# Four hand-written orders of work made anew in a fused attention, FFN and routed-expert kernel

## The chip, the cores and the metric

The kernel runs on one core of one Trainium2 chip. The metric is the device time of one execution in microseconds: the median of the runs of the kernel before is 764.94 us (three runs, 762.08, 764.94 and 765.34).

## What is computed

```python
# attention, B=4, H=8, 512 local and 32 global positions, D=64
s_g = scale * np.matmul(q_g, k_all.transpose(0, 1, 3, 2)); out_g = np.matmul(sm(s_g), v_all)
mask = np.abs(pos[:, None] - pos[None, :]) <= 32          # local queries: a window, and all globals
s_l = np.concatenate([s_lg, np.where(mask, s_ll, -1e9)], axis=-1)
out_l = np.matmul(sm(s_l), np.concatenate([v_g, v_l], axis=2))
x = concatenate([out_g, out_l], axis=2) as (2176, 512) rows
# FFN, 512 to 2048 to 512
x = (np.maximum(x @ w_in, 0.0) ** 2) @ w_out
# routed experts, 8 of 512 to 1024 to 512
xc = x[x @ w_skip > 0]; logits = xc @ w_gate
e_idx = argmax(logits); gate_w = softmax(logits)[e_idx]
out = x.copy(); out[x @ w_skip > 0] = xc + gate_w * (np.maximum(xc @ w1[e], 0) @ w2[e])
```

## The kernel before

The 2176 rows are 16 tiles of 128 local tokens and one tile of the 128 global queries. The FFN takes the local tiles two at a time, in 8 blocks of 256 tokens. Most products are made in two parts: a tensor is split into a high part in float32r and the low rest, and three matmuls (high by high, high by low, low by high) stand for one. Block 0 works in plain float32 while the weights are still arriving. Attention for block j+1 runs beside the FFN of block j, and the routing of block j-1's tiles too. After block 7 the FFN of the global tile, its routing, and the first expert's two tiles follow; then the experts' tiles, under branches on the token counts.

The order of all this is written out by hand in four strings of tokens, each token one step. Every engine executes its instructions in the order in which the tokens emit them, and the DMA queues of SP, ACT and POOL too. SEQ (L21, read by `do`, L897) covers the start: loads, preparation, blocks 0 and 1 of the FFN, attention of tiles 0 to 5. EVEN (L31) is run for blocks 2, 4 and 6, ODD (L36) for 3, 5 and 7 (L953). TAIL (L41) is read by the loop at L997.

The tokens:
- F, E (and I, H in SEQ, which put the low part on VectorE instead of POOL): one FFN unit, alternately a first product (L664 to L666: 12 matmuls of 256 columns) and a second (L685 to L687: 12 of 512). F and I square on VectorE, E and H on ScalarE. The digit in SEQ is the block.
- a, b: a step of local attention for the block's two tiles. Step 1 is the scores (L387: 128 matmuls) with the softmax of one half (L396 to L403), step 2 the softmax of the other half, steps 3 and 4 transposes (L412), step 5 the product with v (L421), step 6 the transposes of the result.
- g: a step of global attention, four steps for each half of the heads: products with the keys (L453), transposes (L473), products with the values (L486: 40 matmuls), transposes of the result. Only the even blocks have them.
- q, 0 to 3, G: transposes of queries and keys. r, s, t: a step of the routing of one tile (t: the global tile): transposes (L270) and a bf16 copy; the other two thirds of the rows (L564 to L566) on VectorE; L586, the logits, and a chain of small VectorE operations; L611, L612 and a second chain that ends in two one-hot matrices (L633, L637); L640, the slot table, and the store of the rows to DRAM.
- W in SEQ: a transfer of 512 KB of FFN weights on SP's queue. A: puts the words of one chunk together, ScalarE (L211) and VectorE (L215, L219, L225). C, D: splits a chunk of weights, the low part on POOL (C) or VectorE (D). V, lv, lk, lq, lg and L: other loads on SP's queue.
- In TAIL: T is a step of the global tile's FFN (six matmuls of 512 columns, some with transposes). X and Y are steps of the first expert's tiles 0 and 1. W and w fetch 512 KB of expert weights, on ACT's queue and on SP's. C and c split a weight; the low part of the weight before (L794) goes to VectorE (C) or POOL (c). O opens places and issues two gathers (L817, POOL's queue), S makes the slot rows, gEJ gathers for expert E's tile J, pEJ transposes and splits what was gathered.

Of the kernel before, what the change touches and what calls it, by code (L numbers as in the profile page):

```python
# [18 lines left out]


SEQ = """  # L21
    Lk00 Lk01 Lg0 W P00 0G P01 Lq0 A L9 W Lq1 03 P0 00 V 0q 01 02 A W P1 0a W 0a W V 0a W A W 0b 0a A V 0b 0a 0b V A
    0a 0b W V W A 0b W A W W 0b 1q V A E0 A I0 W W W A 1a D W A 1a W F0 A 1a A D W E0 W H0 I0 A 1a 1b 1a W V A H0 A
    W H0 D A W E0 W D 1a F0 W 1b I0 Lg1 F0 A D V A W 1b E0 1b W A H0 D 1g A 1b C Lv00 V F0 1g E0 A A H0 H0 E0 A 1b C
    1g D D F0 Lq2 W Lv01 D H0 A 1g V W H1 H1 A A W H0 W H1 Lk10 1g A H1 H0 W 1g F1 2G D V A C C A I1 21 W 1g D H0 D
    E1 20 I0 D A Lq3 D H1 1g F0 A I0 I0 2q Lk11 D C E0 E0 A D 22 E0 C 23 F0 C C E1 R00 2a H1 R00 E1 2a R01 H1 2a R00
    R01 E1 I1 F1 C R00 2b R01 F1 2a D F1 2b 2a F1 V Lv10 D F1 H1 R01 R00 A D 2b H1 H1 C 2a I1 C E1 C V H1 F1 2b C I1
    F1 I1 H1 R01 2b E1 D 2b H1 V V
"""

EVEN = """  # L31
    E E q E a r a F E r E s E r E E s g E a s E a E a g F F r a F lg r V E g lv1 b s F g F E F b F F b b F E s V F
    lk1 V E g b F g F b g F F F g lq lk0 V F
"""

ODD = """  # L36
    q E E E G E 3 0 F E 2 r lq E r 1 F F r E a lv0 r E F s F r E s a F s a F F E b F a b F s E E a F E b V V b E E b
    a F F V s E b F F F V
"""

TAIL = """  # L41
    w T T r T r r s T T s T s W r w T T r T s C C T c s w T T T C W O W T c C W T p00 C w C T p01 w W T W W X X
    t C X t X t C X X t c X X X t S g02 g10 X Y Y Y W W Y W W p02 p10 Y W W Y Y W Y Y Y Y
"""

WARM = 8
# [1071 lines left out]
```

## Time and profile before

| | |
|---|---|
| median of 3 runs | 764.94 us |
| the profiled execution | 761.9 us, span 760.2 us |
| TensorE matmul busy | 720.3 us (95%) |
| TensorE weight load busy | 595.3 us (78%) |
| VectorE, ScalarE, POOL busy | 425.6, 394.9, 178.1 us |
| mean granted clock of TensorE | 0.991 |
| DMA | 95.32 MB, mean 125 GB/s |

Busy time is the sum of an engine's instruction times; weight loads run beside matmuls. The span goes from the first to the last instruction. A timeline row says in brackets how long the engine stood idle before the instruction and what ended that; "issue" means that no semaphore did. From 171.80 us on, a block of the main loop takes 59 to 65 us; block 7 ends at 528.90, and the experts behind the branches begin at 594.60.

### The profile page before, as it was taken

Reading aid. Unit: us, or ns where it says so; the run is one execution under the profiler, and the core shown is the slowest. Engines: PE = TensorE matmul, PEld = TensorE weight load, DVE = VectorE, ACT = ScalarE, POOL = GpSimd, SP = SyncE. Lnnn points to the kernel's source line nnn. Section 1 sums busy time; section 2 is a strip of 40 time slices with the busy share of each in tenths; the row PEclk is TensorE's granted clock in tenths of the full one; section 3 lists DMA queues with packets and bytes.
Section 4 is the critical chain, followed back from the end, with each engine's and each line's share of the span. In section 5 each row is a group of like instructions: output and inputs, shape, how many; then the busy total and the mean of one; then the engine's idle time right before and its main releaser. Section 6 shows DMA issues by size and latency. Waiting matters only on the chain. (4 is left out here: it accounts for less than half of the span.)

```text
span 760.2 us, 18565 instructions
## 1 busy us (share of the span) xinstructions
PE 720.3 (95%) x7443; PEld 595.3 (78%) x7443; DVE 425.6 (56%) x1072; ACT 394.9 (52%) x970; POOL 178.1 (23%) x209
## 2 busy tenths in 40 slices
PE   6789999999899999999999999999889998999897
PEld 4566776888788989878988888888577777887775
DVE  2889894954551652753174464241875289327881
ACT  5767566546345554533654634433453277326771
POOL 5000033231111111111212111221032243414431
PEclk9899999999999999999999999999999999999999
DMA  9999921142525113063304050001473699417700
GB/s 271 228 331 259 242 71 35 41 102 42 127 66 125 35 33 78 19 148 79 79 31 102 2 150 30 28 29 44 152 250 106 241 328 325 149 48 258 275 26 30
DMA packets 117396, 95.32 MB, mean 125 GB/s; under 512 B 83125, under 2 KB 90293, under 8 KB 117284
## 3 DMA queue, kind: packets, MB, share of 16 engines
q1 hardware_dynamic: 105856, 69.50, 34.2%
q10 hardware_dynamic: 8548, 16.00, 6.1%
q0 software_dynamic: 2880, 8.33, 3.3%
q8 instruction: 69, 1.13, 0.6%
q14 instruction: 43, 0.35, 0.1%
HBM read 82.08 MB, written 12.85 MB: 125 GB/s over the span
## 5 line engine op out<-in xcount | busy, mean ns | idle before, releaser
L176 POOL TENSOR_TENSOR gl<-g,gh 128x256 fp32r<-128x256 f32 x105 | 79.6, 758 | 339.4 <-ACT gh L175 177.7
L664 PE MATMUL h<-xh,w_in 128*128 128x256 f32 x448 | 131.1, 293 | 0.0
L666 PE MATMUL h<-xh,w_in 128*128 128x256 f32 x448 | 125.2, 279 | 0.0
L665 PE MATMUL h<-xl,w_in 128*128 128x256 f32 x448 | 125.2, 279 | 0.0
L685 PE MATMUL acc<-w_out,gh 128*128 128x512 f32 x224 | 93.5, 417 | 0.3 <-issue 0.3
L668 ACT ACTIVATE g<-h 128x256 f32<-128x256 f32 x128 | 48.7, 380 | 85.6 <-PE h L666 66.0
L687 PE MATMUL acc<-w_out,gl 128*128 128x512 f32 x224 | 88.7, 396 | 0.1
L686 PE MATMUL acc<-w_out,gh 128*128 128x512 f32 x224 | 88.4, 395 | 0.0
L664 PEld LDWEIGHTS h<-xh,w_in 128*128 128x128 f32 x448 | 84.1, 188 | 3.6 <-ACT gh L700 0.3
L665 PEld LDWEIGHTS h<-xl,w_in 128*128 128x128 f32 x448 | 84.3, 188 | 2.1 <-issue 0.3
L666 PEld LDWEIGHTS h<-xh,w_in 128*128 128x128 f32 x448 | 84.0, 188 | 0.0
L403 ACT ACTIVATE sm<-sm,mx 128x128 f32<-128x128 f32 x128 | 49.9, 391 | 64.5 <-DVE mx L401 62.9
L175 ACT CAST gh<-g 128x256 fp32r<-128x256 f32 x112 | 45.4, 406 | 29.0 <-DVE g L698 26.9
L396 DVE TENSOR_TENSOR sm<-sc,mask 128x512 f32<-128x512 f32 x32 | 21.9, 686 | 60.2 <-PE sc L387 56.6
L687 PEld LDWEIGHTS acc<-w_out,gl 128*128 128x128 f32 x224 | 42.0, 188 | 11.6 <-POOL gl L176 1.2
L176 DVE TENSOR_TENSOR ehl<-ertr,ehl 128x512 fp32r<-128x512 f32 x28 | 19.4, 692 | 50.8 <-ACT ehl L175 50.8
L685 PEld LDWEIGHTS acc<-w_out,gh 128*128 128x128 f32 x224 | 42.1, 188 | 6.9 <-issue 0.8
L686 PEld LDWEIGHTS acc<-w_out,gh 128*128 128x128 f32 x224 | 42.2, 188 | 5.8 <-issue 0.3
L848 ACT ACTIVATE er<-eh 128x512 f32<-128x512 f32 x28 | 16.7, 598 | 44.4 <-PE eh L845 44.4
L698 DVE TENSOR_TENSOR g<-h,g 128x256 f32<-128x256 f32 x46 | 19.3, 419 | 31.5 <-ACT g L668 31.3
L683 PE MATMUL acc<-st_raw_out,gh 128*128 128x512 f32 x64 | 31.6, 615 | 2.8 <-DVE st_raw_in L215 2.8
L817 POOL DMA_INDIRECT xg<-x2d,slots x20 | 24.2, 1208 | 38.2 <-DVE xp L176 8.6
(701 smaller groups left out, 1631.2 us busy)
## 6 DMA issues: line engine op xcount, KB each, us to landing
st_e<-in_moe_w_dram SPq DMA_DIRECT2D x50, 512.0 KB, 7.7
vr<-in_v_l_dram SPq DMA_DIRECT2D x56, 192.0 KB, 4.5
st_raw_in<-in_moe_w_in_dram SPq DMA_DIRECT2D x16, 512.0 KB, 9.4
st_raw_out<-in_moe_w_out_dram SPq DMA_DIRECT2D x16, 512.0 KB, 7.5
st_e<-in_moe_w_dram ACTq DMA_DIRECT2D x14, 512.0 KB, 7.0
x2d<-x ACTq DMA_DIRECT2D x17, 256.5 KB, 2.9
st_gv<-in_v_l_dram SPq DMA_DIRECT2D x8, 512.0 KB, 4.8
out_dram<-x ACTq DMA_DIRECT2D x16, 256.0 KB, 3.3
```

Source lines behind the costliest of these rows:

```text
L175: nc.scalar.copy(hi, src)
L176: (lo_engine or nc.vector).tensor_tensor(out=lo, in0=src, in1=hi.bitcast(F32), op=ALU.subtract)
L403: nc.scalar.activation(sm[:, hh, :], sm[:, hh, :], AF.Exp, bias=mx[:, hh:hh + 1], scale=SCALE, accum_out=osum[:, 2 * hh + g:2 * hh + g + 1],)
L664: nc.tensor.matmul(h, lhsT=wh, rhs=xh[:, k, :], start=(k == 0), stop=False)
L665: nc.tensor.matmul(h, lhsT=wh, rhs=xl[:, k, :], start=False, stop=False)
L666: nc.tensor.matmul(h, lhsT=wl, rhs=xh[:, k, :], start=False, stop=(k == KD - 1))
L668: nc.scalar.activation(g, h, AF.Relu)
L683: nc.tensor.matmul(acc[z], lhsT=gh[:, c], rhs=w, start=(f == 0), stop=(f == KF - 1))
L685: nc.tensor.matmul(acc[z], lhsT=gh[:, c], rhs=wh, start=(f == 0), stop=False)
L686: nc.tensor.matmul(acc[z], lhsT=gh[:, c], rhs=wl, start=False, stop=False)
L687: nc.tensor.matmul(acc[z], lhsT=gl[:, c], rhs=wh, start=False, stop=(f == KF - 1))
L817: nc.gpsimd.indirect_dma_start(out=gathered(e, j), out_offset=None, in_=x2d, in_offset=bass.IndirectOffsetOnAxis(ap=gi, axis=0), bounds_ch ...
```

## The change

Only the four strings change. No operation is added or taken away. In SEQ block 1 has six H fewer, three F and three E more, block 0 one F and two E fewer, two I and one H more. EVEN holds the same tokens in another order; ODD has two E in the place of two F; TAIL has one c in the place of a C and two w in the place of two W. In EVEN only a load (lv1) stands before between the third g (L486) and the first b (scores); after, "E r V E lv1 F" stands there. In TAIL the steps of the routes stand further apart, with more T's between them, O stands earlier among the T's, and the low parts that go to POOL are other ones.

```diff
 SEQ = """
-    Lk00 Lk01 Lg0 W P00 0G P01 Lq0 A L9 W Lq1 03 P0 00 V 0q 01 02 A W P1 0a W 0a W V 0a W A W 0b 0a A V 0b 0a 0b V A
-    0a 0b W V W A 0b W A W W 0b 1q V A E0 A I0 W W W A 1a D W A 1a W F0 A 1a A D W E0 W H0 I0 A 1a 1b 1a W V A H0 A
...
+    Lk00 Lk01 Lg0 W P00 P01 0G 03 Lq0 A W Lq1 P0 L9 00 0q 01 02 A W W W P1 W V V 0a 0a 0a A 0b A 0a V 0b 0a 0b 0b V
+    A 1q A 0a W W W 0b D W A 0b V W A F0 A V W W I0 W W Lg1 W A 1a A 1a F0 V D A 1a W A W W H0 I0 F0 D A 1a 1b 1a E0
...
 EVEN = """
-    E E q E a r a F E r E s E r E E s g E a s E a E a g F F r a F lg r V E g lv1 b s F g F E F b F F b b F E s V F
-    lk1 V E g b F g F b g F F F g lq lk0 V F
+    q E F F r E r a F a E lg F s F r E s E F g a s E a E a g F F r V a F g E r V E lv1 F b g s E F b E E b E V g b F
+    b F b F b F g F s lk1 F g E V g lq F lk0 E
 """
 ODD = """
-    q E E E G E 3 0 F E 2 r lq E r 1 F F r E a lv0 r E F s F r E s a F s a F F E b F a b F s E E a F E b V V b E E b
-    a F F V s E b F F F V
+    q E F lq G E 3 2 F 1 E F r E r 0 E r F a r lv0 F s E E r s E E s a E a E F F b b F a F F a b E b a F V s F V E b
+    E V b V E s E F F E E
 """
 TAIL = """
-    w T T r T r r s T T s T s W r w T T r T s C C T c s w T T T C W O W T c C W T p00 C w C T p01 w W T W W X X
-    t C X t X t C X X t c X X X t S g02 g10 X Y Y Y W W Y W W p02 p10 Y W W Y Y W Y Y Y Y
+    r W r w w T T s r s T T c T s T T r T T s r C T W w s O T W T C C T T W c C T W p00 c p01 T c T X w W X w t C t
+    X w X t X Y W t X X X C t S Y W X w Y g02 Y g10 Y Y C W W p10 X Y Y Y W Y Y W p02
 """
```

## Rows read from the trace of the kernel before

**Rows 1.** Page, part 1: busy us (share of the span) and instructions of TensorE.

```profile
PE 720.3 (95%) x7443; PEld 595.3 (78%) x7443; DVE 425.6 (56%) x1072; ACT 394.9 (52%) x970; POOL 178.1 (23%) x209
```

**Rows 2.** Table by stages: stretch, its length, busy us of each engine, clock, DMA.

```profile
core 0: us, PE busy (x) PEld busy (x) DVE busy (x) ACT busy (x) POOL busy (x), PEclk, DMA share, GB/s
0.00:36.82 36.82, 24.94 (x457) 17.41 (x457) 19.36 (x42) 23.29 (x60) 11.01 (x46) 0.91 1.00 246
...
171.80:236.90 65.10, 62.62 (x867) 53.91 (x866) 32.10 (x112) 29.24 (x96) 11.74 (x16) 1.00 0.36 80
236.90:295.90 59.00, 59.00 (x768) 52.55 (x767) 25.46 (x86) 32.09 (x95) 11.79 (x16) 1.00 0.29 71
295.90:360.20 64.30, 62.42 (x867) 54.17 (x866) 32.00 (x111) 29.25 (x96) 11.74 (x16) 1.00 0.31 70
...
528.90:594.60 65.70, 57.32 (x299) 44.28 (x298) 41.73 (x113) 25.65 (x43) 14.39 (x9) 0.97 0.57 184
```

**Rows 3.** Waits of TensorE in the main loop: total us, times, longest.

```profile
PE sc L387 <- issue: 4.4, 3, 2.2
```

**Rows 4.** Table by stages, short stretches from L486 or a first score on.

```profile
203.97:208.73 4.76, 2.57 (x169) 2.13 (x168) 0.35 (x1) 0.42 (x2) 0.72 (x1) 1.00 0.75 179
327.34:332.02 4.68, 2.80 (x170) 2.44 (x169) 0.35 (x1) 0.40 (x1) 0.73 (x1) 1.00 0.98 239
450.63:453.63 3.00, 2.67 (x169) 2.35 (x168) 0.35 (x1) 0.39 (x1) 0.73 (x1) 1.00 0.90 245
177.16:179.66 2.50, 2.21 (x133) 1.93 (x132) 0.75 (x2) 0.55 (x2) 0.73 (x1) 1.00 0.00 0
269.73:271.28 1.55, 1.55 (x130) 1.51 (x129) 0.00 (x0) 0.14 (x1) 0.73 (x1) 1.00 0.00 0
```

**Rows 5.** Timeline of TensorE, block 2: start, us, line, idle before.

```profile
204.80 1.36 PE L387 MATMUL sc<-kT,qT 64*32 64x96 f32 x100
208.35 0.45 PE L387 MATMUL sc<-kT,qT 64*32 64x96 f32 x28 [2.19 <-issue]
```

**Rows 6.** Timeline of TensorE, block 3: the 12 matmuls of one FFN unit.

```profile
271.28 0.38 PE L664 MATMUL h<-xh,w_in 128*128 128x256 f32 x1
...
272.80 0.60 PE L412 MATMUL ptr<-ident,sm 128*128 128x128 f32 x4
```

**Rows 7.** Page, part 3: the instruction queue, its packets and MB.

```profile
q8 instruction: 69, 1.13, 0.6%
```

**Rows 8.** Waits of TensorE between 528.9 and 594.7.

```profile
PE pl L586 <- DVE x2T L565: 2.2, 2, 1.3
PE pt L640 <- DVE ohl L637: 2.2, 2, 1.9
PE pl L586 <- DVE x2T L566: 1.6, 3, 0.5
PE eh L843 <- issue: 1.2, 1, 1.2
```

**Rows 9.** Timeline of TensorE, behind block 7: two of the waits.

```profile
552.23 0.33 PE L640 MATMUL pt<-ohs,ohl 128*128 128x136 f32 x1 [1.90 <-DVE ohl L637]
...
571.26 0.41 PE L586 MATMUL pl<-w,x2T 128*128 128x27 bf16 x10 [0.54 <-DVE x2T L566]
```

**Rows 10.** Timeline of VectorE, behind block 7.

```profile
544.68 0.16 DVE L631 SCALAR_TENSOR_TENSOR rt<-rt 128x1 f32<-128x1 f32 x1
...
549.53 2.13 DVE L631 SCALAR_TENSOR_TENSOR rt<-rt 128x1 f32<-128x1 f32 x1
...
565.45 1.21 DVE L794 TENSOR_TENSOR e7l<-st_e,e7h 128x1024 fp32r<-128x1024 f32 x1
```

**Rows 11.** Timeline of POOL in the same stretch.

```profile
549.28 2.36 POOL L794 TENSOR_TENSOR e1l<-st_e,e1h 128x1024 fp32r<-128x1024 f32 x1 [22.18 <-ACT e1h L788]
```

**Rows 12.** Table by stages, TensorE alone, behind the route's wait.

```profile
572.50:576.00 3.50, 3.50 (x12) 0.51 0.00 0
```

**Rows 13.** Timeline of TensorE in the start.

```profile
44.84 1.06 PE L683 MATMUL acc<-st_raw_out,gh 128*128 128x512 f32 x2 [2.85 <-DVE st_raw_in L215]
```

**Rows 14.** Page, part 6: transfers of FFN weights: count, KB each, us to landing.

```profile
st_raw_in<-in_moe_w_in_dram SPq DMA_DIRECT2D x16, 512.0 KB, 9.4
```

More of the change, by code (lines that the diff above doesn't have):

```diff
@@ L21 @@
 SEQ = """
-    Lk00 Lk01 Lg0 W P00 0G P01 Lq0 A L9 W Lq1 03 P0 00 V 0q 01 02 A W P1 0a W 0a W V 0a W A W 0b 0a A V 0b 0a 0b V A
-    0a 0b W V W A 0b W A W W 0b 1q V A E0 A I0 W W W A 1a D W A 1a W F0 A 1a A D W E0 W H0 I0 A 1a 1b 1a W V A H0 A
-    W H0 D A W E0 W D 1a F0 W 1b I0 Lg1 F0 A D V A W 1b E0 1b W A H0 D 1g A 1b C Lv00 V F0 1g E0 A A H0 H0 E0 A 1b C
-    1g D D F0 Lq2 W Lv01 D H0 A 1g V W H1 H1 A A W H0 W H1 Lk10 1g A H1 H0 W 1g F1 2G D V A C C A I1 21 W 1g D H0 D
-    E1 20 I0 D A Lq3 D H1 1g F0 A I0 I0 2q Lk11 D C E0 E0 A D 22 E0 C 23 F0 C C E1 R00 2a H1 R00 E1 2a R01 H1 2a R00
@@ L27 @@
-    R01 E1 I1 F1 C R00 2b R01 F1 2a D F1 2b 2a F1 V Lv10 D F1 H1 R01 R00 A D 2b H1 H1 C 2a I1 C E1 C V H1 F1 2b C I1
-    F1 I1 H1 R01 2b E1 D 2b H1 V V
+    Lk00 Lk01 Lg0 W P00 P01 0G 03 Lq0 A W Lq1 P0 L9 00 0q 01 02 A W W W P1 W V V 0a 0a 0a A 0b A 0a V 0b 0a 0b 0b V
+    A 1q A 0a W W W 0b D W A 0b V W A F0 A V W W I0 W W Lg1 W A 1a A 1a F0 V D A 1a W A W W H0 I0 F0 D A 1a 1b 1a E0
+    A A H0 V D W H0 W D W 1a E0 C 1b A F0 I0 A A 1b F0 W 1b I0 A 1g V A 1b H0 1g A H0 Lv01 H0 A D I0 H0 W C C D E0 D
@@ L29 @@
+    1b Lv00 1g W A H0 1g A W F1 F1 1g W A W A H0 H1 Lq2 A E0 E1 1g I1 Lk10 W 2G D W D F1 V A D D A W 1g H0 E0 I1 I0
+    20 A H1 W C F0 A 2q Lk11 Lq3 C C H0 D C I0 A 21 E0 C 22 I0 23 E1 E0 D R00 C 2a E1 V R00 E1 2a R01 E1 R00 2a R01
+    E1 F1 E1 A C R00 2b H1 R01 2a F1 F1 2b 2a D F1 R00 R01 F1 V H1 1g C D C H1 H1 2b C D 2b F1 D E1 D 2b 2a E1 Lv10
+    R01 F1 V I1 F1 I1 D H1 2b V I1 V
 """
 EVEN = """
-    E E q E a r a F E r E s E r E E s g E a s E a E a g F F r a F lg r V E g lv1 b s F g F E F b F F b b F E s V F
@@ L33 @@
-    lk1 V E g b F g F b g F F F g lq lk0 V F
+    q E F F r E r a F a E lg F s F r E s E F g a s E a E a g F F r V a F g E r V E lv1 F b g s E F b E E b E V g b F
+    b F b F g F s lk1 F g E V g lq F lk0 E
 """
 ODD = """
-    q E E E G E 3 0 F E 2 r lq E r 1 F F r E a lv0 r E F s F r E s a F s a F F E b F a b F s E E a F E b V V b E E b
-    a F F V s E b F F F V
+    q E F lq G E 3 2 F 1 E F r E r 0 E r F a r lv0 F s E E r s E E s a E a E F F b b F a F F a b E b a F V s F V E b
+    E V b V E s E F F E E
```

## The prediction

> **What bounds the kernel now.** I read the busy table first: TensorE's matmul row holds 95% of the span [rows 1]. So there are only some 40 us in which TensorE stands, and an order of work can win nothing else, except where the same matmuls run at the lower clock. The table by stages [rows 2] is next; it tells where those 40 us lie. The blocks of the main loop are the thing to compare: the odd block 236.90 to 295.90 lasts 59.00 us and TensorE is busy for all 59.00, the even block before it lasts 65.10 with 62.62 busy and the one behind it 64.30 with 62.42. (An even block has the global attention in addition, so it is longer by right; that it stands for 2.48 and 1.88 us is not.) The stretch behind the last block, which TAIL orders, lasts 65.70 with 57.32 busy: 8.4 us of standing, the densest in the kernel. The start loses most (36.82 with 24.94 busy), but there the DMA share is 1.00 at 246 GB/s: the inputs set it, not the order.
>
> Third view, who waits for whom in the loop: 4.4 us, three times, in front of the scores of L387, and the releaser is given as "issue", that is, no semaphore [rows 3]. The timeline shows one: scores begin at 204.80 right behind L486 (the products of the global queries), 100 of the 128 run, then 2.19 us pass, then the other 28 [rows 5]. Measured as whole stretches from the first L486 (or the first score) to what follows, four places take 4.76, 4.68, 3.00 and 2.50 us [rows 4]. The fifth row there is an odd block's scores with no L486 ahead: 1.55 us for 128, no stop.
>
> What are these stops? Matmuls and weight loads are separate instructions, so L486 with 40 matmuls and the scores with 128 are 336 instructions in about 2.4 us, while an FFN unit is 12 matmuls and 12 loads in about 1.5 us (271.28 to 272.80) [rows 6]. The 16 KB packets of the instruction queue, 69 of them [rows 7], show that the program is streamed in during the run. My reading: the stop is TensorE outrunning its own instruction supply, which happens only where two dense bunches of small matmuls stand back to back. That is an inference; the row says no more than "not a semaphore".
>
> **The change, part by part.** The counts of the work tokens don't change in sum for TensorE: the same units, steps and transposes. Only order, some choices of engine (six H of block 1 go, three F1 and three E1 come; two F of ODD become E; one C of TAIL becomes c; two W become w), and the place of transfers.
>
> EVEN. Before, the third global step (L486) is followed at once by b, whose first step is the scores. After, the string between them is "E r V E lv1 F": three FFN units and a route step. Three units are 72 instructions in about 4.5 us [rows 6], longer than any of the stops with their scores. By the inference the supply catches up. Price of the four places: L486 takes 0.83 (from 203.97, where the stretch of [rows 4] begins, to the scores' start at 204.80 [rows 5]) and the scores 1.55 [rows 4], so 2.4 is the floor. 4.76, 4.68 and 3.00 lose 2.4, 2.3 and 0.6; the fourth, 2.50, is scores and four transposes with a floor of about 1.9 (1.55, and 0.1 for each transpose by the pitch of [rows 6]), and loses 0.6. Sum 5.9. Against it stand more changes between kinds of work, from 18 runs of non-FFN work to 20 in each of EVEN and ODD, six blocks: 12 changes. An odd block with all 59.00 us busy [rows 2] prices a change at about nothing; a bound from the other side is 0.1 us (the 271.28 unit takes 1.52 where 12 matmuls at its neighbours' pitch would be 1.4 [rows 6]), 1.2 in all. I take 0.4, nearer the row with no idle. Loop: 5.5 us gained, between 2 and 6. ODD's two squares that move from VectorE to ScalarE cost nothing while ScalarE works 32.09 of 59.00 us [rows 2].
>
> TAIL. TensorE's waits in the stretch are 2.2 and 1.6 us for the thirds (L565, L566) in front of L586, 2.2 for the one-hot (L637) in front of L640, and 1.2 at the entry to the branches [rows 8].
> - Thirds. Between a route's transposes and its L586 stood one T (r), or a C (t). After: r1, r2, T, T, s1, r3; then s2, T, T, T, s3; then t1, C, t2, X, X, t3. A T or X is six 512-column matmuls, about 1.5 us by twice the pitch of [rows 6]. The first two get 1.5 us or more of cover beyond what they had, about the longest wait of one route (1.3 and 0.5 together); the third still has one of C's subtractions (1.21 us on VectorE [rows 10]) in front of the thirds, and keeps about 0.6. So 3.8 becomes 0.6: 3.2 gained.
> - One-hot. The long one ended at 552.23 [rows 9]. VectorE's L631 took 2.13 us at 549.53 where it takes 0.16 at 544.68 [rows 10], and ended when a POOL subtraction (e1l, 549.28, 2.36 us) ended [rows 11]: the two engines don't run these side by side. After, that subtraction is a C's, on VectorE, behind the route's chain. 2.2 becomes 0.5: 1.7 gained.
> - Clock. From 572.50 to 576.00 the granted clock is 0.51, the 1.2 GHz level, right after the wait that ends at 571.26 [rows 9, 12]. 3.50 us there are 1.8 at the full clock: 1.7 gained if the wait goes.
> - What the order adds. The subtractions on POOL are now those of the later c's, near p00, p01 and the first X: they can hold a VectorE instruction as e1l did, 2.0 us each. L631 is not among those queued beside them, and two of the three lie near a VectorE chain that leads to TensorE, so I take 0.4 of 0 to 4. The two gathers of O go three T's sooner in TensorE's count, but they still wait for the route's one-hot and its stores; p01, whose data came just in time behind more work, is needed sooner: 0.2, my estimate. p02 is now the last token before the branches, with a ScalarE and VectorE split behind it: 0.2.
> Sum of TAIL: 3.2 + 1.7 + 1.7 - 0.4 - 0.2 - 0.2 = 5.8 gained; between 1.8 (all 4 of POOL's) and 8 (8.4 idle less 1.2 at the branches, and nearly all of the clock's 1.7).
>
> This is where a page's rule can be laid beside the rows. The Trainium skill ("SBUF — State Buffer", section "Who interferes with whom") says that a VectorE instruction with two SBUF inputs and a GpSimd one that reads SBUF exclude each other for the whole instruction, whoever starts first winning. L631 has two SBUF inputs and ended within 0.02 us of e1l: the trace agrees. By it the new c's would cost up to their full 4 us, if a chain of VectorE stood behind each; that is rival 2.
>
> SEQ. The first FFN unit still stands behind eight A's, twelve a/b entries and 11 instead of 12 weight transfers; the new part is that all of block 1's query preparation and more of A's ScalarE work come sooner. TensorE stands for 2.85 us up to 44.84 anyway [rows 13], which absorbs a start that is 1 us late. The whole wait gone would be 2.85 gained, a second of its kind 2.85 lost; I take 0.3 lost, near neither, between -1.5 and +3.
>
> Behind 594.60 the work isn't touched: 0, ±1.
>
> **Sum.** 0.3 - 5.5 - 5.8 = -11.0 us. The profiled run took 761.9 (span 760.2, 1.7 outside it), so 750.9 on its scale; it lies 3.0 under the median of the runs, 764.94, from which the same sum gives 753.9.
>
> **Rivals.**
> 1. The stops aren't supply, or move with the boundaries of the supply to another place of the new order. For it: nothing in the rows names the cause, and EVEN still has scores right behind other work. Against: at four places they follow dense bunches, and the odd block's scores alone show none. Loop +0.4, TAIL and SEQ as above: 764.94 - 5.8 + 0.3 + 0.4 = 759.8. The Trainium skill ("Runtime: NRT & Kernel Launch", section "Instruction fetch mechanics") says that an engine's sequencer fetches the next 16 KB block while it executes the present one, and that the cost is mostly hidden. If that held here, the stops had another cause and this rival would be right; the 2.19 us without a semaphore speak against it.
> 2. The tail gives its gain back: POOL's three subtractions hold VectorE for 2 us each [rows 10, 11], the waits return at p01, the thirds of t or the turns of X, and the clock falls again behind them. TAIL 0, loop and SEQ as above: 764.94 - 5.5 + 0.3 = 759.7.
> 3. Slower: SEQ's weights. From the 24th transfer on, a W stands 0 to 4 FFN units ahead of the A that rebases its chunk; before it was 3 to 10. A transfer takes 9.4 us from issue to landing [rows 14]. If SyncE issues it only about when its turn comes (no free buffer), ScalarE stands at the rebase for about 5 us (9.4 less two units), softmax and squares are queued behind it, and TensorE waits for these. With nine such chunks, three or more exposed cost 15 us and eat the whole gain: 764.94 - 11 + 15 = 769. It decides when buffers come free: there are 36, and by the order the ones that chunks 24 to 28 take were released some ten or more FFN units earlier, so SyncE should run far ahead. I give it little.
> 4. The loop's and the tail's gain are both lost (rivals 1 and 2 together): 765.6, no change.
>
> **How the numbers follow.** My forecast 0.68; rival 1: 0.11; rival 2: 0.11; rival 3: 0.06; rival 4: 0.04. Half a percent, 3.8 us, is about what a measurement of this kernel can tell. Forecast and the two halves at 759.7 are faster by more than that (761.1 is the bound), save for a few cases of the halves in which SEQ loses 2 more: faster 0.85, same 0.09, slower 0.06. The range: below, SEQ's -1.5 instead of 0.3, TAIL's 8, the loop's 6: not all at once, 748.5; above, the halves with 1.5 of SEQ's loss, 761.5.
>
> **What would show it.** Right: the scores behind L486 in blocks 2, 4 and 6 take 1.55 us each with no "issue" wait, and the blocks at 171.80 and 295.90 shrink to about 62.1 and 62.0; the tail shrinks to about 60 with the granted clock at 1.00 throughout; L631 at 0.16 us in both of its routes. Wrong: waits by "issue" in front of other small matmuls of an even block (rival 1); VectorE instructions of 2 to 3 us beside POOL's and waits for the thirds as before (rival 2); ScalarE waiting for st_raw transfers in 60 to 115 us (rival 3). A start of the main loop (171.80) that is off by more than 3 us would break the SEQ term.

## The result, and the profile after

The changed kernel takes 757.46 us (median of 16 runs, 756.29 to 762.52); the kernel before, run beside it, 767.84 (16 runs, 762.08 to 772.55). The ratio is 0.9885, 95% interval 0.9864 to 0.9906: 8.8 us faster, between 7.2 and 10.4. The forecast was 11.0 us, and 753.9 (counted from the median of 764.94).

The two profiled executions tell less of this than one would think: that of before took 761.9 us, 5.9 below its median, that of after 760.46, 3.0 above its own. They differ by 1.4 us. So what follows goes by stages, and by more than one profile where there are several.

Part 1 of the page of after, as [rows 1]:

```profile
PE 721.3 (95%) x7443; PEld 597.2 (79%) x7443; DVE 426.2 (56%) x1079; ACT 392.7 (52%) x962; POOL 178.7 (24%) x210
```

The table by stages of after, as [rows 2] (stretch, its length, busy us of TensorE, weight load, VectorE, ScalarE, POOL, then clock and DMA): blocks 2, 3 and 4, and the stretch behind block 7.

```profile
176.16:238.49 62.33, 62.33 (x868) 54.09 (x867) 32.35 (x112) 29.12 (x96) 11.80 (x16) 1.00 0.34 77
238.49:297.37 58.88, 58.88 (x767) 52.71 (x766) 26.09 (x88) 31.35 (x93) 11.74 (x16) 1.00 0.29 69
297.37:359.81 62.44, 62.44 (x867) 54.19 (x866) 32.31 (x111) 29.14 (x96) 11.79 (x16) 1.00 0.32 76
...
529.12:592.71 63.59, 56.42 (x298) 44.47 (x297) 37.29 (x113) 25.98 (x42) 12.93 (x9) 0.95 0.60 198
```

An even block has no idle TensorE left: length and busy time are the same number. The six blocks together, in the same view of before and then of after:

```profile
171.80:528.95 357.15, 352.46 (x4457) 309.49 (x4456) 161.80 (x573) 172.18 (x525) 70.62 (x96) 1.00 0.26 65
```

```profile
176.16:529.12 352.96, 352.46 (x4457) 310.05 (x4456) 164.60 (x579) 169.30 (x519) 70.59 (x96) 1.00 0.25 64
```

TensorE works 352.46 us in both. The loop's gain is idle time alone, 4.2 us in this pair. But block 2 begins 4.4 us later than before (176.16 for 171.80), and the tail is only 2.1 us shorter (63.59 for 65.70), with the clock at 0.95. The timeline of block 2 after shows the place where the stop of [rows 5] was:

```profile
207.30 0.65 PE L486 MATMUL gpo<-st_gv,gpT 128*32 128x64 f32 x32
207.88 0.31 PE L486 MATMUL gpo<-vgr,gpTg 32*32 32x64 f32 x8
...
212.66 1.73 PE L387 MATMUL sc<-kT,qT 64*32 64x96 f32 x128
```

Some 4.5 us of other work lie between L486 and the scores, and the 128 scores come in one piece. TensorE's waits behind block 7, as [rows 8]:

```profile
PE etr L270 <- DMA xg<-x2d,g: 5.2, 2, 4.8
PE eh L843 <- ACT xp L175: 0.7, 1, 0.7
PE etr L270 <- DMA xg<-x2d,slots: 0.6, 1, 0.6
PE pt L640 <- DVE count L627: 0.3, 1, 0.3
```

The waits for the thirds are gone and the one for the one-hot is 0.3 us; a new one of 4.8 us stands at their side. In the timeline of TensorE it is p00 (the transposes of the first gathered rows); p00 itself, p01 and a T (six matmuls) then run slowly:

```profile
560.39 1.08 PE L270 MATMUL etr<-ident,xg 128*128 128x128 f32 x4 [4.78 <-DMA xg<-x2d,g]
561.90 1.09 PE L270 MATMUL etr<-ident,xg 128*128 128x128 f32 x4 [0.43 <-DMA xg<-x2d,g]
562.64 0.78 PE L743 MATMUL acc<-w_out,gh 128*128 128x512 f32 x1
```

and the table by stages has the 1.2 GHz level behind it, as [rows 12] had it elsewhere:

```profile
560.28:565.20 4.92, 4.38 (x14) 3.56 (x15) 2.00 (x3) 3.04 (x4) 2.08 (x1) 0.51 0.26 96
```

### The profile page after: what moved, and what is told of

Same layout as the page of the kernel before. It is cut to its first block, busy times and chain, and to the rows that moved or that the text cites. A ratio compares the mean times of both kernels' runs of the same rounds, so it can differ in the third digit from the quotient of the medians.

```text
span 758.8 us, 18575 instructions
## 1 busy us (share of the span) xinstructions
PE 721.3 (95%) x7443; PEld 597.2 (79%) x7443; DVE 426.2 (56%) x1079; ACT 392.7 (52%) x962; POOL 178.7 (24%) x210
## 5 line engine op out<-in xcount | busy, mean ns | idle before, releaser
L698 DVE TENSOR_TENSOR g<-h,g 128x256 f32<-128x256 f32 x52 | 21.8, 418 | 82.1 <-ACT g L668 82.1
L683 PE MATMUL acc<-st_raw_out,gh 128*128 128x512 f32 x64 | 33.3, 644 | 4.1 <-issue 4.1
```

The source lines that it names most:

```text
L683: nc.tensor.matmul(acc[z], lhsT=gh[:, c], rhs=w, start=(f == 0), stop=(f == KF - 1))
```

## The experiments

The ratio is to the kernel before, run beside each; a median is of 4 to 16 runs.

| kernel | median us | ratio | 95% interval |
|---|---|---|---|
| changed kernel | 757.46 | 0.9885 | 0.9864 to 0.9906 |
| EVEN alone | 757.89 | 0.9864 | 0.9812 to 0.9915 |
| ODD alone | 766.71 | 1.0012 | 0.9981 to 1.0043 |
| SEQ alone | 768.91 | 1.0019 | 0.9983 to 1.0054 |
| TAIL alone | 764.07 | 0.9951 | 0.9916 to 0.9986 |
| changed, b behind g again | 765.10 | 0.9982 | 0.9958 to 1.0006 |
| before, b two units later | 764.42 | 0.9950 | 0.9925 to 0.9976 |
| changed, SEQ of before | 756.84 | 0.9849 | 0.9812 to 0.9885 |
| changed, later transfers | 754.08 | 0.9818 | 0.9772 to 0.9864 |
| the same, SEQ of before | 754.47 | 0.9815 | 0.9788 to 0.9841 |
| the same, other boundaries | 753.27 | 0.9796 | 0.9767 to 0.9824 |

**The four strings, one at a time.** Each is the kernel before with one string of the changed one. (The diff under "The change" shows one "b F" too many in the second line of the new EVEN: the kernel has "b F b F g F s lk1 ...", so that the tokens are those of before in another order.)

> The kernel before with the changed EVEN alone. My theory (TensorE outruns its instruction supply where L486 and the scores stand back to back): no wait of the scores by 'issue' in the three even blocks, these blocks 2.4, 2.3 and 0.6 us shorter than in the profile of before, 4 to 6 us in all. Rival (the gain of the whole change comes from elsewhere, the tail): under 2 us, and waits by 'issue' in front of other instructions of the even blocks.

EVEN alone is 1.4% faster, as much as the whole change. No wait of TensorE is left in its loop. Two of its even blocks in the table by stages:

```profile
174.03:236.26 62.23, 62.23 (x868) 54.01 (x867) 32.43 (x112) 29.13 (x96) 11.76 (x16) 1.00 0.39 86
295.19:357.58 62.39, 62.39 (x867) 54.15 (x866) 32.32 (x111) 29.14 (x96) 11.79 (x16) 1.00 0.33 76
```

The rival falls: neither is the gain under 2 us nor is there a new wait. That the timed gain (10.4 us, 6.5 to 14.4) is larger than the 4 to 6 expected is taken up below.

> The kernel before with the changed ODD alone. Theory: odd blocks had no idle of TensorE, their new order changes nothing: within 1.5 us of the kernel before, odd blocks of 58.9 us as before. Rival: two squares moved to ScalarE and the new spacing make new waits of 0.3 us and more, odd blocks over 59.5 us.

Nothing measurable; its odd block lasts 59.04 us for 59.00. The theory holds.

> The kernel before with the changed SEQ alone. Theory: the start loses what the two profiles show, block 2 begins at about 176 us instead of 171.8, so 3 to 5 us slower. Rival (the start of the one profiled run was an unlucky one): within 1.5 us, block 2 begins at 171 to 173 us.

The timing can't tell it from no change (from 0.2% faster to 0.5% slower). Its block 2 begins at 173.15 us in its own profile, so neither theory nor rival is met cleanly. Over all the profiles in which nothing else of the start differs, block 2 begins at 173.2 us on average with the old SEQ (eight, 171.25 to 174.76) and at 175.2 with the new one (four, 173.15 to 176.16).

> The kernel before with the changed TAIL alone. Theory: the waits for the thirds and the one-hot go (about 5 us), the new wait of p00 for its gather takes 5 of 7 us back: 1 to 3 us faster, p00 stands 4 to 6 us and the clock falls behind it. Rival (the gather's wait comes from where the changed SEQ and loop leave the DMA queues): p00 stands less than 1 us and the kernel is 5 to 7 us faster.

3.8 us faster by the timing (1.1 to 6.5), 64.58 us from block 7 to the branches in its profile for 65.70 before. p00 waits 4.1 us here too, so the wait belongs to TAIL and not to what SEQ and the loop leave on the queues.

**Is the stop a matter of instruction supply?** The kernel before, with 64 more instructions ahead of everything:

```diff
         warm(WARM)
+        o = ps.tile([P, DM], F32, tag="x2", bufs=2, name="shift")
+        for _ in range(32):
+            nc.tensor.matmul(o[:, 0:16], lhsT=idle[:, 0:P], rhs=idle[:, 0:16], start=True, stop=True)
```

> The kernel before with 32 tiny matmuls (64 instructions with their weight loads, nothing else) behind the warm-up, where TensorE waits for inputs anyway. Supply theory: the place of the stops is a count of instructions, so in blocks 2, 4 and 6 the scores stop 32 matmuls earlier: after about 68, 93 and 91 of 128 instead of 100, 125 and 123, or not at all. Rival (the stop belongs to the scores, their data or their banks): they stop after 100, 125 and 123 as before.

The timeline of TensorE in its blocks 4 and 6 (start, us, line, x count, idle before):

```profile
331.15 1.22 PE L387 MATMUL sc<-kT,qT 64*32 64x96 f32 x93
333.08 0.48 PE L387 MATMUL sc<-kT,qT 64*32 64x32 f32 x35 [0.71 <-issue]
...
452.92 1.56 PE L387 MATMUL sc<-kT,qT 64*32 64x96 f32 x118
455.89 0.27 PE L387 MATMUL sc<-kT,qT 64*32 64x32 f32 x10 [1.41 <-issue]
```

In block 4 the scores stop after 93, as said to the matmul; in the kernel before it was after 125. In block 2 there is no stop. Block 6 misses the number (118, not 91). Counting every instruction of TensorE in the trace from its start (matmuls, weight loads and semaphore instructions) repairs that: in the kernel before 5057 and 8385 instructions lie ahead of the stops of blocks 2 and 4, in this kernel 8385 and 11713 ahead of those of blocks 4 and 6. Each is 193 more than a multiple of 256. (The 0.33 us stop of block 6 in the kernel before, from which I took 123, is at no such place.) A thing that stays with the count of instructions while the work moves by 32 matmuls belongs to the stream of instructions and not to the scores.

The same kernel settles another stop. In [rows 13] L683 stood 2.85 us, and the list gave VectorE's L215 as the releaser. Its place in the count is 1217, again 193 and a multiple of 256. Here, with VectorE's work untouched:

```profile
40.39 1.62 PE L387 MATMUL sc<-kT,qT 64*32 64x96 f32 x128
41.94 2.07 PE L683 MATMUL acc<-st_raw_out,gh 128*128 128x512 f32 x4
```

L683 follows the scores at once. The six blocks of this kernel last 353.8 us in its profile, 3.4 less than in the first profile of before and nearly as short as with the new EVEN, though no token moved. The kernel as a whole was not faster (766.59 us, one run): other boundaries fell into other bunches, 4.6 us ahead of an L683 at 58.6 us and 3.9 in the middle of an L421, and block 2 begins only at 177.6.

A boundary, that is a place at such a count, doesn't make a stop by itself. Over all the traces, 24 boundaries of the six blocks have 256 instructions ahead of them that began within 2.2 us. Fourteen of them stop TensorE for 0.7 to 3.4 us, and in the 2 us ahead of each the DMA engines are busy at a share of about 0.7 and more; ten cost 0.3 us or less, at a share under 0.4. No boundary with more time than that stops in the loop. So the stops go with busy DMA queues as well as with dense bunches; no run moved the transfers alone to test that.

**Is it the one token?** The changed kernel with b back behind the third g:

```diff
-... V a F g E r V E lv1 F b g s ...
+... V a F g b E r V E lv1 F g s ...
```

> The changed kernel with one token moved: the first b of EVEN stands right behind the third g again (no FFN unit between L486 and the scores), all else as changed. Supply theory: the stops return, 1 to 4 us in each of the three even blocks, 4 to 9 us slower than the changed kernel, so close to the kernel before. Rival (the rest of the new EVEN, its spacing of the other steps, brings the gain): within 1 us of the changed kernel, blocks of 62.4 us.

The gain is gone: 0.9982, with the interval reaching 1. The stops are back; TensorE's waits in its loop and block 2 in the timeline:

```profile
PE sc L387 <- issue: 5.1, 2, 3.2
```

```profile
207.41 1.41 PE L387 MATMUL sc<-kT,qT 64*32 64x96 f32 x99
210.73 0.45 PE L387 MATMUL sc<-kT,qT 64*32 64x96 f32 x29 [1.92 <-issue]
```

Blocks 2 and 4 stop, block 6 doesn't (1.55 us for its scores), so one block fewer than expected. Its block 4:

```profile
300.10:367.38 67.28, 64.06 (x867) 55.52 (x866) 32.09 (x111) 29.23 (x96) 11.75 (x16) 0.97 0.31 70
```

Besides 3.2 us of standing it has 1.6 us more busy time than the 62.44 of after, at a clock of 0.97. So within the new EVEN the place of b is necessary. Is it enough? The kernel before with one token moved:

```diff
-... V E g lv1 b s F g F E F b F F b b F E s ...
+... V E g lv1 s F g F b E F b F F b b F E s ...
```

> The kernel before with one token moved: the first b of EVEN two FFN units and a g step later, all else as before. Theory (the two units between L486 and the scores are the whole of the change's gain): no stop inside the scores of the even blocks, 1.55 us each, 6 to 10 us faster than the kernel before, as much as the changed EVEN alone (0.986) or nearly. Rival: the new EVEN is needed as a whole, the step of b that follows now comes too soon for its softmax and TensorE waits there: 3 us faster or less.

Half right. The scores stand in no block for more than 0.3 us, but the gain is 0.5% (3.8 us), and the rival names why: TensorE waits in new places. In its waits of the loop, and in the timeline of block 2, where eight transposes (0.3 to 0.4 us a set of four elsewhere) take 2.05 us while the softmax comes in piece by piece:

```profile
PE pr L611 <- DVE rt L613: 1.4, 3, 0.5
```

```profile
217.68 2.05 PE L412 MATMUL ptr<-ident,sm 128*128 128x128 f32 x8
```

Its even blocks last 64.53, 64.43 and 63.78 us where EVEN alone has 62.23 to 62.48. The separation removes the stop; the rest of the new EVEN keeps TensorE from waiting for the softmax instead.

**Why is the timed gain larger than the stops of the first profile?**

> The kernel before once more, unchanged, for a second profile. Its profile shown so far took 761.9 us, near the lowest of its 19 timed runs, whose median is 767.9. Theory (the stops of the supply vary with what the DMA queues carry): the even blocks stop for longer, 7 to 10 us over the three, and the start is later. Rival: the blocks are as in the first profile and the difference lies behind 528.9 us.

Its block 4, in the timeline, and the 3.5 us behind the stop in the table by stages:

```profile
331.90 0.25 PE L387 MATMUL sc<-kT,qT 64*32 64x32 f32 x3 [2.75 <-issue]
```

```profile
331.90:335.40 3.50, 3.50 (x22) 3.17 (x22) 3.04 (x17) 1.62 (x9) 0.00 (x0) 0.69 0.79 172
```

In the first profile the same stop was 1.88 us and the 3.56 us behind it ran at 1.00. Here it is 2.75 and the clock falls behind it. Its six blocks together:

```profile
171.25:530.53 359.28, 354.17 (x4457) 310.76 (x4456) 161.82 (x573) 172.29 (x525) 70.70 (x96) 1.00 0.26 65
```

Against the first profile that is 2.1 us more, 1.7 of it busy time: matmuls at the lower clock. The three even blocks lose 7.4 us in all (64.73, 66.89 and 62.64, for about 62.3 each), the low end of the 7 to 10 that I expected. The start isn't later, and the tail is longer too, 67.47 us for 65.70, so the rival has a part of it. Five profiles with the old EVEN (this one, the first, TAIL, SEQ and ODD alone) have 357.15 to 361.08 us for the six blocks, 358.8 on average; six with the new one 352.13 to 353.24, 352.9 on average. So the loop's gain is 5.9 us, with far less scatter after the change than before it. Why the stops differ from one execution of a program to the next isn't shown.

**The gathers of the tail.** The changed kernel with the transfers of 512 KB put behind the gathers:

```diff
-... r C T W w s O T W T C C T T W c C T W p00 c p01 T c T X w W X ...
+... r C T s O T W T C C T T c C T p00 c p01 w W T W c W T X w W X ...
```

> The changed kernel with the expert weights' transfers that stand around O in TAIL put behind it: the eighth behind O, the ninth to twelfth behind p01. Theory (the rows' stores and the two gathers share the DMA queues with four to five transfers of 512 KB): the gathers start 2 to 3 us sooner and land in about 5 us, p00 stands under 1.5 us instead of 5.1, the clock stays at 1.00 there, 3 to 6 us faster than the changed kernel. Rival (the gathers are late by the route's own chain): p00 stands 4 us or more, within 1 us of the changed kernel. Second rival: the weights are missing later, X and Y wait for C's, and what is gained goes there.

POOL's timeline, first of the kernel before, then of the changed kernel, then of this one:

```profile
552.08 2.32 POOL L817 DMA_INDIRECT xg<-x2d,g  x1 [0.43 <-DVE ohs L633]
```

```profile
552.02 1.21 POOL L817 DMA_INDIRECT xg<-x2d,g  x1 [24.89 <-PE acc L744]
553.53 1.63 POOL L817 DMA_INDIRECT xg<-x2d,g  x1 [0.30 <-DMA st_e<-in_moe_w_dram]
```

```profile
549.68 1.82 POOL L817 DMA_INDIRECT xg<-x2d,g  x1 [22.90 <-DMA st_e<-in_moe_w_dram]
551.80 1.01 POOL L817 DMA_INDIRECT xg<-x2d,g  x1 [0.30 <-PE acc L745]
```

and TensorE's here:

```profile
555.42 0.63 PE L270 MATMUL etr<-ident,xg 128*128 128x128 f32 x4
558.26 0.63 PE L270 MATMUL etr<-ident,xg 128*128 128x128 f32 x4 [2.21 <-DMA xg<-x2d,g]
```

The first gather starts 2.3 us sooner, the second 1.7, and they land 5.6 and 6.3 us after their issue; p00 doesn't wait, p01 waits 2.2 us. The tail in the table by stages:

```profile
528.77:587.64 58.87, 54.47 (x298) 42.94 (x297) 41.11 (x113) 26.00 (x42) 13.82 (x9) 1.00 0.64 212
```

58.87 for 63.59, of which 2.8 is idle time and 1.95 busy time that the clock gives back (1.00 for 0.95). Timed it is 754.08 us, 0.67 points of the ratio better than the changed kernel: the theory holds, and X and Y wait for no weight. The rows' store, which the gathers follow, shows the same: it lands 5.7 us after its issue in TAIL alone and 5.2 with the old SEQ, where a transfer of 512 KB is issued on its queue 1.0 us ahead of it, and 3.4 us with later transfers and the old SEQ, where none is; in all three the first gather starts 1.0 to 1.2 us behind that landing.

**The best of both.**

> The changed kernel with the SEQ of before. Theory (the changed SEQ costs what its own run showed, some 0.2%, and the changed kernel's start at 176.2 us shows): 1 to 4 us faster than the changed kernel, block 2 begins at 171.5 to 174 us. Rival: no difference, since the stop behind the first scores of block 1 varies more from run to run than the two orders differ.

Block 2 begins at 173.70, and the ratio is 0.9849; its interval and that of the changed kernel overlap.

> Changed EVEN and ODD, the changed TAIL with the expert weights' transfers behind O as in the run before, and the SEQ of before. Theory: the parts add, since they lie in different stretches: 5 us from the later transfers and 1 to 3 us from the old SEQ off the changed kernel, so 749 to 752 us. Rival: the timed gain of the old SEQ is noise, 753 to 755 us.

754.47 us, no better than with the new SEQ: the rival's value, not the theory's. Together with the run before the cost of the new SEQ is not shown by timing; only the profiles have 2 us of it.

> The same, with the 8 warm-up matmuls replaced by 126 tiny ones, 236 instructions more, so that every boundary of the supply falls elsewhere. By the supply theory the wide bunch of block 1's first scores (40 to 42 us) no longer fills the stretch between two boundaries: the 2 to 4 us stop behind it (before the first L683) is gone, the start of block 2 is 1.5 to 3 us earlier, 747 to 750 us, and any stop in the even blocks stays under 1 us. Rival (that stop is the wait for VectorE's st_raw_in that the list of waits names): L683 waits as before, same time as the run beside it.

The timeline of TensorE, scores of block 1 and what follows:

```profile
43.26 1.62 PE L387 MATMUL sc<-kT,qT 64*32 64x96 f32 x128
44.81 1.62 PE L683 MATMUL acc<-st_raw_out,gh 128*128 128x512 f32 x3
```

The stop behind the scores is gone, as the supply theory has it and against the list's VectorE. In its place a boundary falls into the L421 at 30 us, where 1.6 us are lost, and block 2 begins at 173.19 for 174.76. 753.27 us is the lowest median of the study, but not the 747 to 750 expected; against the run beside it (754.47) the intervals overlap.

## Why the prediction was right, and where it was off

**The loop (5.5 us forecast, 5.9 found).** The step held: stops without a semaphore behind L486, priced by the floor of 2.4 us. Blocks 2 and 4 shrank to 62.33 and 62.44 us, where the prediction's sign was about 62. That the stops go with the count of instructions, which I had called an inference, is now shown by the shifted kernel, and that separating the bunches removes them by the token moved back. Two things were missing. The price came from one profile, in which the stops were short; in four others the one in block 4 is 2.75 to 3.4 us (1.80 in a fifth) and the clock falls behind it, which adds 1.6 us of busy time in the two blocks measured. And I took the separation for the whole of the new EVEN, where the kernel with one moved token shows that the spacing behind it matters as much.

Rival 1, with the page's rule behind it, fell. The count of 256 is the block size that the Trainium skill ("Runtime: NRT & Kernel Launch", section "Instruction fetch mechanics") gives, and there the trace agrees; that the cost is mostly hidden doesn't hold here, where one crossing costs up to 3.4 us if the 256 instructions ahead of it take only some 2 us and the DMA queues are busy.

**The tail (5.8 forecast, about 2 found).** The sign set for it, about 60 us at a clock of 1.00 throughout, was missed: 63.59 at 0.95. The thirds and the one-hot went as forecast: waits of 3.8 and 2.2 us became 0 and 0.3. L631 takes 0.16 us at 546.30, and no POOL subtraction held that chain: rival 2's price for the c's was not paid. The step that failed is the sentence on the gathers and on p01, "0.2, my estimate". It measured 5.2 us of waiting and a second fall of the clock (560.28 to 565.20 at 0.51), so that the 1.7 us that I counted for the clock only moved. I had written that the gathers still wait for the stores, and then not priced it. TensorE comes to p00 some 4.7 us sooner (555.6 for 560.28), because its waits are gone; O stands five T's ahead of p00 where it stood two ahead, but the first gather starts at 552.02 as before (552.08), since it follows the rows' store, issued at 545.21. (The row names L744, but with later transfers the gather starts ahead of that matmul.) Then three transfers of weights on SP's queue and two on ACT's are issued between 550.3 and 552.8, and the second gather lands 8.2 us after its issue where it had taken 5.7. What the thirds and the one-hot gave back turned into the wait at p00: in kind that is what rival 2 says of the waits and of the clock, though not by its mechanism. The run with later transfers shows it: 4.7 us back in its profile.

**The start (0.3 loss forecast, 0 to 2 found).** Within the range of -1.5 to 3. By the prediction's own sign, a main loop that starts more than 3 us off 171.80, three of the four profiles with the new SEQ break the term (175.4 to 176.2); but 171.80 was early for the old SEQ too, whose average is 173.2, and the timing shows no loss. But the reason was wrong in one point: the stop of [rows 13] is no slack that absorbs a later start. It is the same shortage of instructions, and in the profile of after it is 4.1 us, with the clock at 0.50 for the 3.7 us behind it. Rival 3 did not come: ScalarE waits for no st_raw transfer between 55 and 120 us, and SEQ alone is within 0.5%.

**ODD** was costed at nothing, and is.

That the sum came out near is in part luck: the tail gave 3.7 us less than its term, and the timed total (8.8 us) is larger than the sum of the average stages (5.9 and 2.1 less 2.0; 8.0 if the start costs nothing, as the timing allows). EVEN alone has the same surplus (10.4 us timed for 5.9). The granted clocks show that the profiles were no average executions: 0.991 in the first profile of before and 0.980 to 0.981 on average in the timed runs of before beside the experiments, 0.976 in the profile of after and 0.983 on average in its timed runs. In which stage the other runs have those 3 to 4.5 us stays open.

Two sums of the prediction don't come out of their terms: the three best ends together give 749.4, so 748.5 is too low for the range's end, and the whole of POOL's price leaves 2.2 us of the tail's gain, not 1.8. The result depends on neither.

## What to carry to other kernels

Where an engine stands and the list names no semaphore, or one that was long given, count the instructions ahead of it: if 32 more small matmuls at the start of the program move the stop by 32, it is the supply, and the cure shown here is work with few instructions between two dense bunches. Look at the DMA share there too: every such stop of the loop had busy queues. Before a load or gather is pulled forward, count the work left between it and its reader, and what else its queue carries at that time; being issued earlier is not landing earlier. And price a stop by several profiles: it costs more than its length when the clock falls behind it.

## What the runs showed of the hardware that was not expected

- In every kernel of this study TensorE's stops of over 0.5 us inside or right behind a bunch of small matmuls, without a semaphore that explains them, stand at 193 (a few at 194) more than a multiple of 256 of its instructions, semaphore instructions counted. They last up to 4.6 us in the start and 0.7 to 3.4 us in the loop.
- In the loop such a place stopped TensorE only where the 256 instructions ahead began within 2.2 us and the DMA share of the 2 us ahead was about 0.7 or more (14 places); at a share under 0.4 ten equally dense ones cost 0.3 us or less.
- A stop of 1.88 us left the clock at 1.00 for the next 3.56 us; one of 2.75 us was followed by 3.50 us at 0.69, one of 4.78 us by 4.92 us at 0.51. The length doesn't decide it alone: behind 2.19 us (block 2 before) the next 3.50 us ran at 1.00, behind 2.06 us (block 2 of SEQ alone) at 0.51.
- The two gathers of 128 rows landed 4.9 and 5.7 us after their issue in the kernel before; with five transfers of 512 KB issued in the 2.5 us around the first, the second took 8.2 in the changed kernel.
